# Transposing q, k and u by DMA transfers on SyncE's queue in a fused ALiBi sliding-window attention and MLP-mixer kernel

## The chip, the cores and the metric

The kernel runs on one core of a Trainium2 chip. The metric is the device time of one execution in microseconds. Three runs of the kernel before took 337.27, 339.14 and 339.30 us; the median is 339.14 us. One further execution was profiled; every row of a trace in this document is from such a profiled execution.

## The reference

For 8 batches of 576 tokens, 8 heads of 64, an attention with a window of 128 keys and a linear distance penalty per head is followed by an MLP mixer over the heads' joined output x (576 x 512 per batch):

```python
scores = scale * np.matmul(q, k.transpose(0, 1, 3, 2))
mask = (rel >= 0) & (rel < window)            # rel = query position - key position, window = 128
scores = np.where(mask, scores + bias[None], -1000000000.0)
attn = np.exp(scores - max); attn = attn / (sum(attn) + 1e-09)
x = np.matmul(attn, v)                        # heads joined: 512 columns
h = np.maximum(xt @ w_tok1, 0.0) @ w_tok2     # xt = x transposed: mixes the 576 tokens through 256
u = x + h.transpose(0, 2, 1)
out = u + np.maximum(u @ w_ch1, 0.0) @ w_ch2  # mixes the 512 channels through 1536
```

## The kernel before

**Blocks.** Two batches form a pair `pr` with nine blocks of 128 tokens: blocks 0 to 3 are the first batch's first 512 tokens, 4 to 7 the second's, and block 8 (`TAIL`) holds the last 64 tokens of both. They are loaded and prepared in the order `ORDER = [0, 1, 2, 3, 7, TAIL, 4, 5, 6]` (L97), 36 blocks in all (`todo`). A batch with an even number attends blocks 0, 1, 2, 3 and TAIL, one with an odd number 4 to 7.

**Loads.** `load` (L80 to L95) fetches a block of q, k and v from memory on GpSimd's (POOL's) queue, cast from f32 to bf16 on the way, with tokens on partitions and heads times 64 in the row. q and k go to rings `qld` and `kld` of 12 buffers each (pool `ld`, L55), v to a ring of 14. `load_to(n + 7)` keeps the issue seven blocks ahead of the block that is being prepared.

**Preparing a block.** Scores need the head dimension on partitions. `transposes` (L190 to L202) turns a block of q and k with eight TensorE transpositions (L195: four squares of 128 x 128 of q, four of k, two heads in each) into one PSUM tile `tp` of pool `ps_o`, which has one buffer (L64), and one VectorE copy (L201) brings it to `qkT` in SBUF (pool `tp` of 8 buffers, L56).

**Attention.** A unit is one block of queries. `scores` (L204 to L234) makes 8, 16 or 24 matmuls into two PSUM tiles `sp` (L219), one for each group of four heads, each from a pool of one buffer (L63): 8 for blocks 0 and 4, which have no earlier keys; 24 for TAIL. ScalarE takes the exponential (L228), VectorE multiplies with a mask that carries the distance penalty (L231). `values` (L236 to L258) multiplies with v for one group of heads into `ot` (L252), again in the one buffer of `ps_o`, and VectorE divides by the sums (L255, L257) into `xb`. `attention` (L262 to L287) runs the units, with the values of a unit behind the scores of the next one.

**Token mix.** `token_mix` (L292 to L335) makes `t1` (L303), its relu on ScalarE (L305), `ht` for each block (L321) and u = x + h on VectorE (L322). Then every block of u is transposed with four TensorE transpositions (L327) into `ut` (pool `ps_o`) and copied by VectorE (L333) to `uT`, or `uTt` for TAIL.

**Channel mix.** `channel_mix` (L338 to L375) makes 12 tiles `ct` with four matmuls each (L347), all of which read `uT` of all four blocks, with a relu on ScalarE (L349); for an odd batch also three `cx` for TAIL (L356) after every fourth `ct`. Then, for each block, 12 matmuls into `o2` (L365, named `o` in the trace), the addition of u on VectorE (L369) into `ob` (three buffers, L61), and a store on SyncE's (SP's) queue (L374, or two halves for TAIL, L372).

**The order of the work.** Attention and token mix of batch 0 run alone. Then, for each batch, `interleave` (L386 to L398) lays the channel mix of batch b and the attention and token mix of batch b + 1 (`side`, L377) into one another. Every `yield` states the cost of a step in nominal ns (450 for a prepared block, 700 for the scores of a unit, 300 for the values of one head group, 225 for a transposed block of u, 864 for a `ct`); as much side work is laid as 0.78 of the channel mix's cost. The framework makes each engine's queue from this, with the waits between engines; the trace shows that it also sets ready matmuls of one group between those of another, so that the queue's order is the listed order only in the large. The last batch's channel mix has no side work beside it.

Of the kernel before, what the change touches and what calls it, by code (L numbers as in the profile page):

```python
# [11 lines left out]
BF16 = mybir.dt.bfloat16  # L12
# [4 lines left out]
def kernel(  # L17
# [15 lines left out]
    nc = tc.nc  # L33
    P = nc.NUM_PARTITIONS
# [9 lines left out]
    NHP = H // 2  # L44
    NJ = DTOK // P
    NCB = DM // P
# [5 lines left out]
    HEADS = [[0, 2, 4, 6], [1, 3, 5, 7]]  # L52

    const = ctx.enter_context(tc.tile_pool(name="const", bufs=1))
    ld = ctx.enter_context(tc.tile_pool(name="ld", bufs=12))  # L55
    tpool = ctx.enter_context(tc.tile_pool(name="tp", bufs=8))  # L56
    ppool = ctx.enter_context(tc.tile_pool(name="pp", bufs=3))
    small = ctx.enter_context(tc.tile_pool(name="small", bufs=4))
    xpool = ctx.enter_context(tc.tile_pool(name="xp", bufs=2))
# [4 lines left out]
    ps_o = ctx.enter_context(tc.tile_pool(name="ps_o", bufs=1, space=PS))  # L64
    ps_m = ctx.enter_context(tc.tile_pool(name="ps_m", bufs=3, space=PS))

    ident = const.tile([P, P], BF16, name="ident")
# [27 lines left out]
        return got  # L95

    ORDER = [0, 1, 2, 3, 7, TAIL, 4, 5, 6]  # L97
    todo = [(pr, blk) for pr in range(B // 2) for blk in ORDER]
    loaded = {}

    def load_to(n):
        while len(loaded) < min(n, len(todo)):
            key = todo[len(loaded)]
            loaded[key] = load(*key)
# [82 lines left out]
    qkT = {}  # L187
    xs = {}

    def transposes(pr, blk):  # L190
        got = loaded[pr, blk]
        tp = ps_o.tile([P, 2 * NHP, P], BF16, name="tp", tag="o")
        for i, t in enumerate(("q", "k")):
            for hp in range(NHP):
                nc.tensor.transpose(  # L195
                    tp[:, i * NHP + hp, :],
                    got[t][:, 2 * hp : 2 * hp + 2, :].rearrange("p h d -> p (h d)"),
                    ident[:, :],
                )
        t = tpool.tile([P, 2 * NHP, P], BF16, name="qkT", tag="qkT")  # L200
        nc.vector.tensor_copy(out=t[:, :, :], in_=tp[:, :, :])  # L201
        qkT[pr, blk] = t  # L202

    def scores(pr, blk):  # L204

        tail = blk == TAIL
        first = 0 if tail or blk % NC else 1
        me = qkT[pr, blk]
        sp = [ps_s[e].tile([P, 4, 2, P], F32, name=f"sp{e}", tag="s") for e in range(2)]

        work = [(1, blk, 0, P)]
        if tail:
            work += [(0, NC - 1, 0, R), (0, 2 * NC - 1, R, P)]
        elif not first:
            work += [(0, blk - 1, 0, P)]
        for i in range(4):
            for kind, kb, c0, c1 in work:
                for e in range(2):
                    nc.tensor.matmul(  # L219
                        sp[e][:, i, kind, c0:c1],  # L220
                        lhsT=qkT[pr, kb][e * D : (e + 1) * D, NHP + i, :],
                        rhs=me[e * D : (e + 1) * D, i, c0:c1],
                        start=True, stop=True,
                    )
        pb = []
        for e in range(2):
            pe = ppool.tile([P, 4, 2, P], BF16, name=f"pe{e}", tag=f"pe{e}")
            nc.scalar.activation(out=pe[:, :, first:, :], in_=sp[e][:, :, first:, :],  # L228
                                 func=ACT.Exp, scale=scale)
            mk = (maskt if tail else masks)[e]  # L230
            nc.vector.tensor_tensor(out=pe[:, :, first:, :], in0=pe[:, :, first:, :],  # L231
                                    in1=mk[:, :, first:, :], op=ALU.mult)
            pb.append(pe)
        return pb  # L234
# [27 lines left out]
    def attention(b):  # L262
        pr, half = b // 2, b % 2
        if half == 0:
            xs[pr] = xpool.tile([P, NB, DM], BF16, name="xb", tag="xb")
        units = SCORE_ORDER[half]
        trs = [ORDER[:6], ORDER[6:]][half]
        n = pr * NB + (6 if half else 0)
        wait = list(trs)
        held = None  # L270
        for u in units + [None]:
            need = [] if u is None else ([u, 2 * NC - 1] if u == TAIL else [u])
            while any((pr, w) not in qkT for w in need):
                t = wait.pop(0)
                n += 1
                load_to(n + 7)
                transposes(pr, t)
                yield 450
            got = None
            if u is not None:  # L280
                got = (u, scores(pr, u))
                yield 700
            if held is not None:
                for e in range(2):
                    values(pr, held[0], e, held[1][e])
                    yield 300
            held = got  # L287


    us, uts, r1s = {}, {}, {}  # L290

    def token_mix(b):  # L292
        pr, half = b // 2, b % 2
        xb = xs[pr]
        if half == 0:
            us[pr] = xpool.tile([P, NB, DM], BF16, name="ub", tag="ub")
        blocks = list(range(half * NC, (half + 1) * NC))
        r1 = rpool.tile([P, NJ, DM], BF16, name="r1", tag=f"r1{half}")
        for j in range(NJ):
            t1 = ps_m.tile([P, DM], F32, name="t1", tag="m")  # L300
            ks = [(c, blocks[c]) for c in range(NC)] + [(NC + half, TAIL)]
            for n, (c, blk) in enumerate(ks):
                nc.tensor.matmul(t1[:, :], lhsT=W1[:, c, j * P : (j + 1) * P], rhs=xb[:, blk, :],  # L303
                                 start=n == 0, stop=n == len(ks) - 1)
            nc.scalar.activation(out=r1[:, j, :], in_=t1[:, :], func=ACT.Relu)  # L305
            yield 1080
        r1s[pr, half] = r1
        uT = rpool.tile([P, NCB, NC * P], BF16, name="uT", tag="uT")
        uTt = None
        if half:  # L310
            blocks.append(TAIL)
            uTt = rpool.tile([P, NCB, P], BF16, name="uTt", tag="uTt")
        for blk in blocks:
            ht = ps_m.tile([P, DM], F32, name="ht", tag="m")
            if blk == TAIL:
                mms = [(W2t[:, i, j, :], r1s[pr, i][:, j, :]) for i in range(2) for j in range(NJ)]
            else:
                c = blk % NC
                mms = [(W2[:, j, c * P : (c + 1) * P], r1[:, j, :]) for j in range(NJ)]
            for n, (l, r) in enumerate(mms):  # L320
                nc.tensor.matmul(ht[:, :], lhsT=l, rhs=r, start=n == 0, stop=n == len(mms) - 1)  # L321
            nc.vector.tensor_tensor(out=us[pr][:, blk, :], in0=ht[:, :], in1=xb[:, blk, :], op=ALU.add)  # L322
            yield 432
        for blk in blocks:
            ut = ps_o.tile([P, NCB, P], BF16, name="ut", tag="o")
            for cb in range(NCB):
                nc.tensor.transpose(ut[:, cb, :], us[pr][:, blk, cb * P : (cb + 1) * P], ident[:, :])  # L327
            if blk == TAIL:
                to = uTt[:, :, :]
            else:  # L330
                c = blk % NC
                to = uT[:, :, c * P : (c + 1) * P]
            nc.vector.tensor_copy(out=to, in_=ut[:, :, :])  # L333
            yield 225
        uts[b] = (uT, uTt)  # L335


# [39 lines left out]
    def side(b):  # L377

        yield from attention(b)
        yield from token_mix(b)  # L380
# [21 lines left out]
    load_to(9)  # L402
    load_channel_weights(1)
    drain(attention(0))
    drain(token_mix(0))
    for b in range(B):
        other = side(b + 1) if b + 1 < B else None
# [31 lines left out]
```

## Time and profile before

| | |
|---|---|
| runs | 337.27, 339.14, 339.30 us, median 339.14 us |
| profiled execution | 335.55 us, span of its instructions 333.8 us |
| mean granted TensorE clock | 0.987 |
| chain that ended last, by engine | PE 84%, DVE 7%, ACT 4%, issue 1%, DMA 1%, POOL 1% |
| q0, transfers issued by POOL | 116640 packets, 17.97 MB |
| q1, transfers issued by SP | 5248 packets, 9.44 MB |

How to read it. PE is TensorE's matmuls (transpositions among them), PEld its weight loads, DVE VectorE, ACT ScalarE, POOL GpSimd, SP SyncE. The span runs from the first to the last instruction; the execution's own time is 1.75 us longer. A row of the groups names a line, an engine and an operation, output and inputs by the program's names, the count, busy us and the mean of one in ns, and the idle time of the engine ahead of it with what ended it. A row of a timeline begins with the start and the duration in us; matmuls are pipelined, so durations of neighbours overlap, and the distance between starts is what a group takes. A table of stretches gives for each piece of the span the busy time of each engine with the count of instructions, the granted clock, and the load of the DMA engines. Answers on one tile end with the time from a transfer's issue to its landing.

### The profile page before, as it was taken

How to read it: one execution, taken by the hardware profiler on the slowest of the kernel's cores; microseconds unless marked ns; L12 is line 12 of the kernel's file. 1: busy time of each engine (PE TensorE's matmuls, PEld its weight loads, DVE VectorE, ACT ScalarE, POOL GpSimd, SP SyncE). 2: the span in 40 equal slices, each digit the busy share in tenths (PEclk: the TensorE clock that was granted, in tenths of full speed). 3: DMA queues.
4: the chain of work that ended last, by engine and by line, in shares of the span. 5: the costliest groups of instructions: out<-in, count | busy, mean ns of one | idle time of the engine just before them, and what ended most of it. 6: DMA issues, size and time to landing. Idle time of an engine off the chain costs nothing.

```text
span 333.8 us, 6457 instructions
## 1 busy us (share of the span) xinstructions
PE 303.6 (91%) x2688; PEld 162.6 (49%) x2688; DVE 169.7 (51%) x378; ACT 136.9 (41%) x213; POOL 111.0 (33%) x146
## 2 busy tenths in 40 slices
PE   2457769999999999999999999999999999999993
PEld 1234335545555555455565555455654555455541
DVE  2354456563665636474656546464656447461021
ACT  1653227702774038602863047504772057404600
POOL 8998565888786033303472000000000000000000
PEclk9999599999999999999999999999999999999998
DMA  9999999999999359914999220011000220011022
GB/s 74 136 114 167 170 195 161 139 117 189 174 105 131 75 110 77 67 44 101 73 85 83 81 78 3 0 63 66 2 2 13 83 63 2 0 65 63 2 76 82
DMA packets 121917, 27.81 MB, mean 83 GB/s; under 512 B 113824, under 2 KB 117280, under 8 KB 121888
## 3 DMA queue, kind: packets, MB, share of 16 engines
q0 software_dynamic: 116640, 17.97, 76.1%
q1 hardware_dynamic: 5248, 9.44, 8.2%
q8 instruction: 21, 0.34, 0.4%
q14 instruction: 8, 0.07, 0.1%
HBM read 35.91 MB, written 9.44 MB: 136 GB/s over the span
## 4 chain that ended last, share of the span: by engine, by line
PE 84%; DVE 7%; ACT 4%; issue 1%; DMA 1%; POOL 1%; POOLq 0%
PE o L365 28%; PE ct L347 23%; PE sp L219 7%; PE tp L195 6%; PE ot L252 6%; PE t L303 5%; PE ht L321 5%; PE cx L356 3%; PE ut L327 3%; ACT pe L228 2%; DVE xb L257 2%; DVE pe L231 2%; DVE ub L322 1%; DMA kld<-in_k_dram 1%; DVE qkT L201 1%
## 5 line engine op out<-in xcount | busy, mean ns | idle before, releaser
L349 ACT ACTIVATE r<-ct 128x512 bf16<-128x512 f32 x96 | 56.0, 601 | 133.9 <-PE ct L347 133.9
L347 PE MATMUL ct<-uT,WC 128*128 128x512 bf16 x384 | 98.0, 379 | 0.5 <-DVE uT L333 0.5
L365 PE MATMUL o<-WC,r 128*128 128x512 bf16 x384 | 95.4, 379 | 0.4
L228 ACT ACTIVATE pe<-sp 128x1024 bf16<-128x1024 f32 (+1 forms) x72 | 63.0, 926 | 27.3 <-PE sp L219 27.3
L365 PEld LDWEIGHTS <-r 128*128 128x128 bf16 x384 | 36.0, 98 | 37.6 <-issue 1.9
L91 POOL DMA_DIRECT2D qld<-in_q_dram x40 | 35.6, 891 | 45.3 <-PE tp L195 39.3
L369 DVE TENSOR_TENSOR ob<-o,ub 128x512 f32<-128x512 f32 x36 | 24.8, 690 | 48.1 <-PE o L365 48.1
L347 PEld LDWEIGHTS <-WC 128*128 128x128 bf16 x384 | 33.5, 98 | 28.0 <-issue 0.6
L231 DVE TENSOR_TENSOR pe<-pe,mask 128x1024 bf16<-128x1024 bf16 (+1 forms) x64 | 39.0, 619 | 12.1 <-ACT pe L228 8.0
L201 DVE COPY qkT<-tp 128x1024 bf16<-128x1024 bf16 x36 | 24.9, 692 | 31.5 <-PE tp L195 31.5
L94 POOL DMA_DIRECT2D v<-in_v_dram x40 | 35.0, 881 | 15.1 <-PE ot L252 6.2
L92 POOL DMA_DIRECT2D kld<-in_k_dram x40 | 35.4, 884 | 8.3 <-DMA WC<-in_moe_w_ch_dram 5.8
L322 DVE TENSOR_TENSOR ub<-ht,xb 128x512 bf16<-128x512 f32 x36 | 24.0, 688 | 27.1 <-PE ht L321 26.7
L252 PE MATMUL ot<-v,pe 128*128 128x65 bf16 (+1 forms) x544 | 30.4, 201 | 6.7 <-DVE pe L231 3.5
L252 PEld LDWEIGHTS <-pe 128*128 128x128 bf16 (+1 forms) x544 | 22.4, 102 | 26.6 <-DVE xb L257 17.1
L257 DVE TENSOR_TENSOR xb<-ot,rt 128x256 bf16<-128x256 f32 x72 | 30.6, 425 | 2.5
L219 PE MATMUL sp<-qkT 64*128 64x128 bf16 (+1 forms) x544 | 24.6, 224 | 4.0 <-DVE qkT L201 3.1
L255 DVE RECIPROCAL rt<-ot 128x4 f32<-128x4 f32 x72 | 12.9, 179 | 26.1 <-PE ot L252 25.5
L219 PEld LDWEIGHTS <-qkT 64*128 64x128 bf16 x544 | 17.6, 98 | 17.6 <-DVE qkT L201 16.6
L303 PE MATMUL t<-xb,W 128*128 128x512 bf16 x80 | 23.4, 402 | 0.8 <-DVE xb L257 0.8
L195 PE MATMUL tp<-ident,qld 128*128 128x128 bf16 x144 | 14.8, 228 | 9.1 <-DMA qld<-in_q_dram 5.0
L321 PE MATMUL ht<-r,W 128*128 128x512 bf16 x64 | 19.4, 398 | 0.3 <-ACT r L305 0.3
(46 smaller groups left out, 179.4 us busy)
## 6 DMA issues: line engine op xcount, KB each, us to landing
out_dram<-ob SPq DMA_DIRECT2D x32, 256.0 KB, 2.0
qld<-in_q_dram POOLq DMA_DIRECT2D x32, 128.0 KB, 5.5
kld<-in_k_dram POOLq DMA_DIRECT2D x32, 128.0 KB, 5.6
v<-in_v_dram POOLq DMA_DIRECT2D x32, 128.0 KB, 5.5
WC<-in_moe_w_ch_dram POOLq DMA_DIRECT2D x4, 768.0 KB, 10.4
out_dram<-ob SPq DMA_DIRECT2D x8, 128.0 KB, 2.3
qld<-in_q_dram POOLq DMA_DIRECT2D x8, 64.0 KB, 4.6
kld<-in_k_dram POOLq DMA_DIRECT2D x8, 64.0 KB, 4.2
```

The lines of the kernel that those rows point to most:

```text
L91: nc.gpsimd.dma_start(out=got["q"][p0 : p0 + n, :, :], in_=rows(q, b, s0, n))
L92: nc.gpsimd.dma_start(out=got["k"][p0 : p0 + n, :, :], in_=rows(k, b, s0, n))
L219: nc.tensor.matmul(sp[e][:, i, kind, c0:c1], lhsT=qkT[pr, kb][e * D : (e + 1) * D, NHP + i, :], rhs=me[e * D : (e + 1) * D, i, c0:c1], sta ...
L228: nc.scalar.activation(out=pe[:, :, first:, :], in_=sp[e][:, :, first:, :], func=ACT.Exp, scale=scale)
L231: nc.vector.tensor_tensor(out=pe[:, :, first:, :], in0=pe[:, :, first:, :], in1=mk[:, :, first:, :], op=ALU.mult)
L252: nc.tensor.matmul(ot[to, i, :], lhsT=l, rhs=r, start=m == 0, stop=m == len(mms) - 1, skip_group_check=True)
L257: nc.vector.tensor_tensor(out=x4[:, :, e, :], in0=ot[:, :, 0:D], in1=rt[:, :, :].broadcast_to([P, 4, D]), op=ALU.mult)
L303: nc.tensor.matmul(t1[:, :], lhsT=W1[:, c, j * P : (j + 1) * P], rhs=xb[:, blk, :], start=n == 0, stop=n == len(ks) - 1)
L321: nc.tensor.matmul(ht[:, :], lhsT=l, rhs=r, start=n == 0, stop=n == len(mms) - 1)
L347: nc.tensor.matmul(ct[:, :], lhsT=WC1[:, cb, t * P : (t + 1) * P], rhs=uT[:, cb, :], start=cb == 0, stop=cb == NCB - 1)
L349: nc.scalar.activation(out=r2[:, t, :], in_=ct[:, :], func=ACT.Relu)
L365: nc.tensor.matmul(o2[:, :], lhsT=l, rhs=WC2[:, t, :], start=t == 0, stop=t == NHT - 1)
```

## The change

Three things are edited.

1. The pool of loaded q and k goes from 12 to 9 buffers each, the pool of `qkT` from 8 to 11.
2. The first six blocks of the order are transposed on TensorE as before. For the other 30, `transpose_to(n + 4)` issues two transposing transfers on SyncE's queue, one for q and one for k, from the loaded tile straight to `qkT`, up to four blocks ahead of the block whose turn it is. For those blocks `transposes`, with its PSUM tile, its copy and its step of cost 450, is not called.
3. For all batches but the first, each block of u is transposed by one transfer on SyncE's queue from `ub` to `uT` or `uTt`; the four transpositions, the PSUM tile, the copy and the step of cost 225 go.

Stores stay on the same queue, and everything else is as it was.

```diff
@@ -52,8 +52,8 @@
     HEADS = [[0, 2, 4, 6], [1, 3, 5, 7]]
 
     const = ctx.enter_context(tc.tile_pool(name="const", bufs=1))
-    ld = ctx.enter_context(tc.tile_pool(name="ld", bufs=12))
-    tpool = ctx.enter_context(tc.tile_pool(name="tp", bufs=8))
+    ld = ctx.enter_context(tc.tile_pool(name="ld", bufs=9))
+    tpool = ctx.enter_context(tc.tile_pool(name="tp", bufs=11))
     ppool = ctx.enter_context(tc.tile_pool(name="pp", bufs=3))
     small = ctx.enter_context(tc.tile_pool(name="small", bufs=4))
     xpool = ctx.enter_context(tc.tile_pool(name="xp", bufs=2))
@@ -95,6 +95,7 @@
         return got
 
     ORDER = [0, 1, 2, 3, 7, TAIL, 4, 5, 6]
+    EARLY = 6
     todo = [(pr, blk) for pr in range(B // 2) for blk in ORDER]
     loaded = {}
 
@@ -200,6 +201,21 @@
         t = tpool.tile([P, 2 * NHP, P], BF16, name="qkT", tag="qkT")
         nc.vector.tensor_copy(out=t[:, :, :], in_=tp[:, :, :])
         qkT[pr, blk] = t
+
+    moved = [EARLY]
+
+    def transpose_to(n):
+
+        while moved[0] < min(n, len(todo)):
+            key = todo[moved[0]]
+            moved[0] += 1
+            t = tpool.tile([P, 2 * NHP, P], BF16, name="qkT", tag="qkT")
+            for i, x in enumerate(("q", "k")):
+                nc.sync.dma_start_transpose(
+                    out=t[:, i * NHP : (i + 1) * NHP, :],
+                    in_=loaded[key][x][:, :, :].rearrange("p h d -> p (h d)"),
+                )
+            qkT[key] = t
 
     def scores(pr, blk):
 
@@ -270,12 +286,14 @@
         held = None
         for u in units + [None]:
             need = [] if u is None else ([u, 2 * NC - 1] if u == TAIL else [u])
-            while any((pr, w) not in qkT for w in need):
+            while any(w in wait for w in need):
                 t = wait.pop(0)
                 n += 1
                 load_to(n + 7)
-                transposes(pr, t)
-                yield 450
+                transpose_to(n + 4)
+                if (pr, t) not in qkT:
+                    transposes(pr, t)
+                    yield 450
             got = None
             if u is not None:
                 got = (u, scores(pr, u))
@@ -322,16 +340,20 @@
             nc.vector.tensor_tensor(out=us[pr][:, blk, :], in0=ht[:, :], in1=xb[:, blk, :], op=ALU.add)
             yield 432
         for blk in blocks:
-            ut = ps_o.tile([P, NCB, P], BF16, name="ut", tag="o")
-            for cb in range(NCB):
-                nc.tensor.transpose(ut[:, cb, :], us[pr][:, blk, cb * P : (cb + 1) * P], ident[:, :])
             if blk == TAIL:
                 to = uTt[:, :, :]
             else:
                 c = blk % NC
                 to = uT[:, :, c * P : (c + 1) * P]
-            nc.vector.tensor_copy(out=to, in_=ut[:, :, :])
-            yield 225
+            if b == 0:
+                ut = ps_o.tile([P, NCB, P], BF16, name="ut", tag="o")
+                for cb in range(NCB):
+                    nc.tensor.transpose(ut[:, cb, :], us[pr][:, blk, cb * P : (cb + 1) * P],
+                                        ident[:, :])
+                nc.vector.tensor_copy(out=to, in_=ut[:, :, :])
+                yield 225
+            else:
+                nc.sync.dma_start_transpose(out=to, in_=us[pr][:, blk, :])
         uts[b] = (uT, uTt)
```

## The prediction, made before the result was known

> **What bounds the kernel now.** I read the page first, then the table of busy time by stretches, cut where each batch's channel mix begins (the first `ct` after the last `o`).
>
> ```profile
> span 333.8 us, 6457 instructions
> PE 303.6 (91%) x2688; PEld 162.6 (49%) x2688; DVE 169.7 (51%) x378; ACT 136.9 (41%) x213; POOL 111.0 (33%) x146
> DMA  9999999999999359914999220011000220011022
> ```
>
> ```profile
> core 0: us, PE busy (x) PEld busy (x) DVE busy (x) ACT busy (x) POOL busy (x), PEclk, DMA share, GB/s
> 0.00:46.50 46.50, 23.57 (x242) 14.58 (x243) 20.79 (x62) 16.17 (x29) 40.04 (x62) 0.93 1.61 138
> 46.50:80.10 33.60, 33.38 (x275) 17.14 (x275) 18.31 (x40) 14.46 (x22) 24.62 (x30) 1.00 2.07 153
> 80.10:120.90 40.80, 40.35 (x399) 22.23 (x398) 23.16 (x49) 17.98 (x27) 22.06 (x27) 1.00 1.52 128
> 120.90:154.30 33.40, 33.18 (x275) 17.04 (x274) 19.00 (x41) 14.46 (x22) 8.77 (x10) 1.00 0.73 72
> ...
> 302.70:333.80 31.10, 26.03 (x157) 13.03 (x154) 4.15 (x6) 8.96 (x15) 0.00 (x0) 0.97 0.15 51
> ```
>
> Three stages. Until 46.5 us PE is half idle: the first batch's attention and token mix run alone. From 46.5 to 302.7 seven channel mixes run with the next batch's attention and token mix between them, and PE is busy 98 to 99% of each (33.18 of 33.40). The last 26 us of work are a channel mix alone. So in the middle, 256 us, work taken off PE is worth its full time unless something else becomes late. DVE and ACT are about half busy there, and the granted clock is 1.00.
>
> **What is removed from PE.** One timeline of PE in the third channel mix gives both kinds of transposition, and a wait that matters below.
>
> ```profile
> 121.58 0.39 PE L195 MATMUL tp<-ident,qld 128*128 128x128 bf16 x4
> 121.80 0.39 PE L195 MATMUL tp<-ident,kld 128*128 128x128 bf16 x4
> 122.03 1.03 PE L347 MATMUL ct<-uT,WC 128*128 128x512 bf16 x4
> ...
> 130.39 0.62 PE L219 MATMUL sp<-qkT 64*128 64x128 bf16 x16
> 130.94 0.42 PE L252 MATMUL ot<-v,pe 128*128 128x65 bf16 x8
> ...
> 132.44 1.19 PE L219 MATMUL sp<-qkT 64*128 64x128 bf16 x16
> 133.56 0.42 PE L252 MATMUL ot<-v,pe 128*128 128x65 bf16 x8
> ...
> 146.47 0.39 PE L327 MATMUL ut<-ident,ub 128*128 128x128 bf16 x4
> 146.69 0.81 PE L365 MATMUL o<-WC,r 128*128 128x512 bf16 x3
> ```
>
> Durations overlap, so I count from start to start. A block of q and k takes PE from 121.58 to 122.03, 0.45 us for eight transpositions; a block of u 146.47 to 146.69, 0.22 us for four. Removed are 30 blocks of q and k (36 less the first six) and 32 of u (36 less batch 0's four): 30 x 0.45 + 32 x 0.22 = 13.5 + 7.0 = **20.5 us**, nearly all between 46.5 and 302.7. An upper bound comes from the chain that ended last:
>
> ```profile
> PE o L365 28%; PE ct L347 23%; PE sp L219 7%; PE tp L195 6%; PE ot L252 6%; PE t L303 5%; PE ht L321 5%; PE cx L356 3%; PE ut L327 3%; ACT pe L228 2%; DVE xb L257 2%; DVE pe L231 2%; DVE ub L322 1%; DMA kld<-in_k_dram 1%; DVE qkT L201 1%
> ```
>
> 6% of 333.8 us x 30/36 plus 3% x 32/36 is 16.7 + 8.9 = 25.6 us; that holds the slow first six blocks too, so I keep 20.5.
>
> **What is removed from DVE.** The copies out of PSUM:
>
> ```profile
> L201 DVE COPY qkT<-tp 128x1024 bf16<-128x1024 bf16 x36 | 24.9, 692 | 31.5 <-PE tp L195 31.5
> L333 DVE COPY uT<-ut 128x512 bf16<-128x512 bf16 x32 | 13.5, 422 | 9.2 <-PE ut L327 9.2
> ```
>
> 30 x 0.692 + 32 x 0.42 = 34 us of DVE. I cost it at nothing: DVE is half idle in the middle, and PE's waits there (0.2 to 0.45 us per stretch) leave almost nothing to win. The tiles `tp` and `ut` also leave the single buffer of ps_o to `ot`.
>
> **A wait that comes back.** The two groups of `sp` above are alike, sixteen matmuls each. The first takes 0.55 us from start to start (130.39 to 130.94); the second, the only full unit of its batch with no block transposed ahead of it, takes 1.12 (132.44 to 133.56). ACT shows why:
>
> ```profile
> 131.04 1.94 ACT L228 ACTIVATE pe<-sp 128x1024 bf16<-128x1024 f32 x2 [0.60 <-PE sp L219]
> 132.87 0.60 ACT L349 ACTIVATE r<-ct 128x512 bf16<-128x512 f32 x1
> 133.62 1.94 ACT L228 ACTIVATE pe<-sp 128x1024 bf16<-128x1024 f32 x2 [0.15 <-PE sp L219]
> ```
>
> Scores have one buffer per head group; the exponentials of the unit before hold it until 131.04 + 1.94 = 132.98, and PE waits in the middle of its group, counted as busy. It costs 0.57 us. Without blocks of 0.45 us between, and with the steps of cost 450 gone so that less channel mix is laid between two units, every full unit can meet it. Full units are three per odd batch (one pays already) and four per even batch: 4 x 2 + 3 x 4 = 20 new ones, at most 20 x 0.57 = 11.4 us. The lower bound is zero: other ready matmuls can fill the place. I take the middle, **5.7 us**.
>
> **What is added on SP's queue.** 30 x 2 + 32 = 92 transposing transfers of 128 x 512 bf16, 128 KB each, among the 40 stores. The trace has no such transfer. Nearest are SP's own stores:
>
> ```profile
> L374 SPq DMA_DIRECT2D out_dram<-ob x3: 333/337/378, 70.7 to 78.3; - x3
> ...
> DMA to landing us min/median/max: 5.8/5.9/6.1
> ```
>
> ```profile
> L374 SPq DMA_DIRECT2D out_dram<-ob x4: 332/332/333, 183.3 to 193.3; - x4
> L372 SPq DMA_DIRECT2D out_dram<-ob x2: 473/530/588, 195.9 to 196.4; - x2
> ...
> DMA to landing us min/median/max: 2.0/2.0/2.4
> ```
>
> The first answer is for 46 to 80 us, while loads fill the DMA engines; the second for 160 to 200 us. An issue holds SP 0.33 to 0.59 us and lands after 2.0 us in quiet time, 5.9 us among loads. Bounds for what one transfer costs the queue: 0.33 us (issue only, transfers overlap) to 5.9 us (one at a time, among loads). The store of the shared block shows two issues at 195.9 and 196.4 us, the second before the first can have landed, so transfers of this queue overlap; I take a holding time well under 2 us and a landing of 2 to 6 us.
>
> Is that covered? A pair of batches takes 74.2 us now (33.4 + 40.8) and would take about 68; it carries 27 transfers and ten stores. At 2.0 us one after another that is 54 + 4 us, still inside. Latency comes from PE's timeline:
>
> ```profile
> 144.96 1.03 PE L321 MATMUL ht<-r,W2t 128*128 128x512 bf16 x4
> 145.82 0.81 PE L365 MATMUL o<-WC,r 128*128 128x512 bf16 x3
> ...
> 154.14 1.03 PE L347 MATMUL ct<-uT,WC 128*128 128x512 bf16 x4
> ...
> 156.41 0.40 PE L219 MATMUL sp<-qkT 64*128 64x128 bf16 x8
> ...
> 174.33 0.63 PE L219 MATMUL sp<-qkT 64*128 64x128 bf16 x24
> ```
>
> Blocks of q and k are issued four ahead of their use. The tightest is within an even batch's attention: block 7 is issued with unit 0 (156.41) and used by the shared unit (174.33), 18 us later; less six blocks on PE (2.7 us) and their lost steps (6 x 450 / 0.78 = 3.5 us), 12 us remain for the four transfers in front. For u, this batch's last `ht` ends at 145.82, 8.5 us before the next channel mix; the lost steps end the side work 3 x 450 / 0.78 = 1.7 us earlier and five `ut` (1.1 us) go, so about 9 us remain. The last transfers alone have to fit there, since each block starts as it is ready. Queued behind a late transfer are the stores; `ob` has three buffers at 2.6 us of `o` each. Price in the middle: zero.
>
> The Trainium skill speaks against this. "VectorE: DVE Perf Modes", The three transpose paths, gives 1309 ns for 128 x 128 through DMA against 390 ns on TensorE; the trace disagrees on the latter, at 55 ns from start to start here. If the former were a rate, a transfer of four squares would take an estimated 5.2 us, 92 of them 482 us, and the kernel would be far slower. "DMA: Bandwidth & Descriptors", Latency and other measured facts, gives 261 GB/s for transposing transfers, an estimated 0.5 us each and 46 us in all, which would leave everything covered. No run here shows either yet.
>
> **Loads, and the start.** The ring of q and k loads shrinks from 12 to 9 buffers, and a load now waits for a transfer on SP nine blocks back instead of PE's work twelve back.
>
> ```profile
> L195 PE MATMUL tp<-ident,qld x144: 216/219/314, 4.8 to 277.6; 128*128 128x128 bf16 x144
> L91 POOL DMA_DIRECT2D qld<-in_q_dram x40: 677/881/1607, 1.3 to 174.0; - x40
> ...
> DMA to landing us min/median/max: 2.5/5.2/12.2
> ```
>
> The last load is issued at 174.0 us and used at 277.6, so loads have up to 100 us of lead and I cost the ring at nothing. Only the start is tight: the ninth block of the order (its k issued at 37.49 us) lands by 49.7 us at the worst 12.2, and two transfers at 5.9 us can end at 61 us, where the scores that use it stand at 56.17 us today.
>
> ```profile
> 37.49 0.87 POOL L92 DMA_DIRECT2D kld<-in_k_dram  x1 [2.86 <-DMA WC<-in_moe_w_ch_dram]
> ...
> 56.17 0.62 PE L219 MATMUL sp<-qkT 64*128 64x128 bf16 x16
> ```
>
> That is 0 to 5 us; channel-mix matmuls fill part of it. I take **1.5 us**.
>
> **The sum.** The profiled execution took 335.55 us (span 333.8). 335.55 - 20.5 + 5.7 + 1.5 = 322.3 us. The median shown, 339.14, lies 3.6 above that execution, so on its scale **326 us**, 4% less.
>
> **The rivals.** *Full gain.* Other matmuls fill every place and the start costs nothing: 335.55 - 20.5 = 315.1, on the median's scale 319; with the chain's 25.6, 314. For it: PE idles 2 us in all of the middle. Against: the 1.12 us group.
>
> *ACT takes the bound.* All 20 units pay 0.57 us and the start its 5 us: 335.55 - 20.5 + 11.4 + 5 = 331.5, on the median's scale 335; with a shortage like it at token mix as well, 336 to 338, no change to be told. For it: exponentials of a full unit hold ACT 1.94 us, and the lost steps crowd them. Against: ACT is 43% busy in those stretches.
>
> *The queue becomes the bound (slower).* Transposing transfers go one at a time on SP. Then a pair of batches needs 27 t + 4 us, and it is slower than before once that passes 74.2 us, from t = 2.6 us. At t = 3.9 us, midway between the stores' 2.0 and 5.9, 92 transfers and 40 stores of 0.4 us take 375 us; from 38 us, when the first loads concerned have landed, and with the last channel mix of 31 us behind them, 38 + 375 + 31 = 444 us. For it: 5.9 us among loads, DMA engines at 90% or more for the first 117 us. Against: the overlapping stores, and loads that end at 174 us. The Trainium skill's 1309 ns (same page and section as above) is this case by rule: an estimated 38 + 482 + 16 + 31 = 567 us.
>
> *It does not do what it says:* the transfers' waits on SP reorder PE's work so that nothing is gained; nothing in the profile speaks for it.
>
> **Chances.** Forecast 0.55 (its own range 320 to 333 us), full gain 0.16, ACT 0.13, the queue 0.14, the last 0.02. A measurement of this kernel tells about 1% from no change, 335.7 to 342.5 us. Faster by more: 0.55 + 0.16 = 0.71; within: 0.13 + 0.02 = 0.15; slower: 0.14. The range 314 to 342 us leaves out the queue's case and a little below: under 0.2.
>
> **What would show it.** Right: PE's `tp` falls to 48 matmuls and `ut` to 16, the even and odd stretches shorten from 33.4 and 40.8 us to about 32 and 38, PE stays above 95% busy there, SP's queue waits for DVE more than for its own transfers. The ACT term: groups of sixteen `sp` of about 1.1 us at most full units. Wrong: PE waiting for DMA at `sp` or at the first `ct` of a batch, transfers landing one behind the other at over 2.6 us, or stores issued late. A shorter first 46.5 us would also be unforeseen, since nothing there changes.

## The result, and the profile after

The changed kernel is slower: 359.19 us median (358.64 to 359.56) against 338.31 (337.27 to 339.3) for the kernel before in the same comparison, a ratio of 1.062 (95% interval 1.057 to 1.066). The forecast was 326 us. The profiled execution took 359.56 us, against 335.55 before. One of the four executions of the last kernel below ran in a slower state of the chip (332.42 us), and its figures are those of the other three.

The page of the changed kernel, the lines that answer to those of before:

```profile
span 357.8 us, 5827 instructions
PE 290.5 (81%) x2279; PEld 150.4 (42%) x2320; DVE 138.4 (39%) x316; ACT 137.4 (38%) x213; POOL 110.7 (31%) x146
PEclk9999555669985699999999999999999999999999
DMA  9999999999999999999993993312300331043012
...
L369 PE MATMUL ct<-uT,WC 128*128 128x512 bf16 x364 | 99.1, 393 | 17.2 <-DMA uT<-ub 15.1
L235 PE MATMUL sp<-qkT 64*128 64x128 bf16 (+1 forms) x544 | 33.1, 233 | 19.6 <-DMA qkT<-kld 15.8
```

PE has 13 us less to do (303.6 to 290.5) and waits much longer. Waits for transfers are new: 15.1 us at one `ct`, and 15.8 us in three waits at `sp`. The DMA engines are full for the first 21 of the 40 slices instead of the first 13, and the granted clock falls to 0.5 to 0.6 in two places (slices of 8.9 us: from 36 to 80 us, and from 107 to 125). Where the time goes is plain from the same table of stretches as before, cut at each batch's channel mix:

```profile
core 0: us, PE busy (x) PEld busy (x) DVE busy (x) ACT busy (x) POOL busy (x), PEclk, DMA share, GB/s
0.00:72.40 72.40, 29.98 (x295) 18.53 (x300) 23.72 (x68) 21.18 (x35) 49.72 (x73) 0.78 1.80 138
72.40:117.60 45.20, 29.90 (x171) 13.13 (x175) 11.51 (x26) 9.87 (x16) 26.90 (x33) 0.80 1.98 153
117.60:157.10 39.50, 38.39 (x329) 20.25 (x336) 17.63 (x39) 18.05 (x27) 21.04 (x26) 0.95 2.02 164
157.10:188.30 31.20, 30.79 (x227) 15.08 (x230) 15.36 (x33) 14.51 (x22) 9.01 (x11) 1.00 1.71 168
188.30:226.30 38.00, 36.91 (x330) 19.99 (x334) 17.63 (x39) 17.91 (x27) 4.04 (x5) 1.00 0.64 98
...
```

From 157 us on the kernel is what was forecast: stretches of 31.2 and 38.0 us where 33.4 and 40.8 stood. The loss lies ahead of that. The first channel mix begins at 72.4 us instead of 46.5 (+25.9), and the first stretch after it contains the wait of 15.1 us. From each kernel's first channel mix to its end, without that wait, the changed kernel is 17.0 us shorter (270.3 against 287.3 us; the expectations below say 16.8). 335.55 + 25.9 + 15.1 - 17.0 = 359.55 us: this is bookkeeping from the two traces, not a check of their causes. A part of the 25.9 us is work moved and not time lost: the first stretch holds 295 matmuls where it held 242, scores of batch 1 that came behind it before.

PE's timeline shows both losses, and, further on, a wait that the prediction had named:

```profile
24.96 0.63 PE L321 MATMUL t<-xb,W 128*128 128x512 bf16 x1 [6.24 <-DMA W<-in_moe_w_tok_dram]
...
49.92 0.39 PE L235 MATMUL sp<-qkT 64*128 64x128 bf16 x2 [10.02 <-DMA qkT<-kld]
...
56.84 0.71 PE L235 MATMUL sp<-qkT 64*128 64x128 bf16 x10 [3.48 <-DMA qkT<-kld]
...
62.30 1.03 PE L235 MATMUL sp<-qkT 64*128 64x128 bf16 x8 [2.26 <-DMA qkT<-kld]
63.27 2.74 PE L339 MATMUL ht<-r,W 128*128 128x512 bf16 x6
...
72.36 1.01 PE L369 MATMUL ct<-uT,WC 128*128 128x512 bf16 x2 [0.51 <-DVE uT L353]
...
117.59 1.87 PE L369 MATMUL ct<-uT,WC 128*128 128x512 bf16 x4 [15.14 <-DMA uT<-ub]
...
159.31 1.09 PE L235 MATMUL sp<-qkT 64*128 64x128 bf16 x16
```

*The start.* The `sp` of 49.92, 56.84 and 62.30 us belong to batch 1, and they stand on PE's queue ahead of batch 0's `ht` (63.27). Before, batch 1's scores came behind batch 0's last `ut`. The scores wait for transferred blocks, 15.8 us in all, and the rest of batch 0's token mix waits behind them. The fourth wait, of a `t` for its weights (6.2 us), is no wait for a transfer: the first of those is issued only at 39.75 us. Here this `t` stands on PE's queue ahead of the scores of block 2; before, it stood behind those of block 3 and did not wait:

```profile
26.47 1.74 PE L303 MATMUL t<-xb,W 128*128 128x512 bf16 x4
```

All six kernels with six early blocks have this wait, of 5.9 to 6.3 us, and none with nine or more. So it comes with another order of PE's queue; why that order changed stays open. The four waits add up to 22.0 of the 25.9 us.

*The wait for u.* What SP does meanwhile is on its own timeline, and DVE's shows when u was ready:

```profile
39.75 1.30 SPq L214 DMA_TRANSPOSE qkT<-qld  x1
41.11 1.26 SPq L214 DMA_TRANSPOSE qkT<-kld  x1
...
102.32 1.25 SPq L214 DMA_TRANSPOSE qkT<-qld  x1
104.10 1.37 SPq L214 DMA_TRANSPOSE qkT<-kld  x1
105.56 6.02 SPq L356 DMA_TRANSPOSE uT<-ub  x4
111.67 1.25 SPq L356 DMA_TRANSPOSE uTt<-ub  x1
113.01 1.56 SPq L396 DMA_DIRECT2D out_dram<-ob  x3
```

```profile
93.63 0.69 DVE L340 TENSOR_TENSOR ub<-ht,xb 128x512 bf16<-128x512 f32 x1 [0.17 <-PE ht L339]
94.93 0.69 DVE L391 TENSOR_TENSOR ob<-o,ub 128x512 f32<-128x512 f32 x1 [0.60 <-PE o L387]
...
119.71 0.69 DVE L391 TENSOR_TENSOR ob<-o,ub 128x512 f32<-128x512 f32 x1 [18.91 <-DMA out_dram<-ob]
```

Batch 1's last u (`TAIL`'s) is ready at 94.3 us, and the transfers of all five blocks are issued from 105.56 on. The first `ob` is ready at 95.6 and its store goes out at 113.01; the fourth `ob` waits 18.9 us for a buffer. From its first transfer at 39.75 us to 105.56, 65.8 us, SP issues 28 transfers of q and k, which hold it 40.6 us in all. Most of the rest it stands at transfers whose blocks have not been loaded:

```profile
SPq L214 <- DMA qld<-in_q_dram: 60.7, 9, 39.1
```

Of these waits (us in total, times, longest), 39.1 us pass ahead of its first transfer, and 21.6 us at eight later ones. The holding alone would not have made u late: an estimate of 28 x 1.3 us from 39.75 on ends at 76 us, before u is there. The order of SP's queue, as its timeline shows it, q and k transfers counted together, then u's, then stores:

```
28 q/k | 5 u | 4 stores | 10 q/k | 4 u | 6 stores | 8 q/k | 5 u | 4 stores | 10 q/k | ...
```

Fourteen blocks, not four, are queued ahead of the first u. They are blocks 6 to 19 of the order, as far as eleven buffers go: block 19 takes over the buffer of block 8, the last of the first pair.

### The profile page after: what moved, and what is told of

Read it like the earlier page. It is cut to its first block, busy times and chain, and to the rows that moved or that the text cites. A ratio compares the mean times of both kernels' runs of the same rounds, so it can differ in the third digit from the quotient of the medians.

```text
span 357.8 us, 5827 instructions
## 1 busy us (share of the span) xinstructions
PE 290.5 (81%) x2279; PEld 150.4 (42%) x2320; DVE 138.4 (39%) x316; ACT 137.4 (38%) x213; POOL 110.7 (31%) x146
## 3 DMA queue, kind: packets, MB, share of 16 engines
q1 hardware_dynamic: 55296, 21.51, 34.1%
## 4 chain that ended last, share of the span: by engine, by line
PE 57%; DMA 19%; POOL 7%; issue 5%; ACT 5%; DVE 4%; SPq 3%; ACTq 0%; POOLq 0%
PE o L387 23%; PE ct L369 16%; DMA qld<-in_q_dram 7%; DMA kld<-in_k_dram 5%; PE ht L339 4%; DMA qkT<-kld 4%; ACT pe L244 4%; PE sp L235 4%; PE ot L268 4%; PE t L321 4%; PE cx L378 2%; DMA uT<-ub 2%; DVE pe L247 2%; POOL v L94 2%; SPq L214 2%
## 5 line engine op out<-in xcount | busy, mean ns | idle before, releaser
L369 PE MATMUL ct<-uT,WC 128*128 128x512 bf16 x364 | 99.1, 393 | 17.2 <-DMA uT<-ub 15.1
L371 ACT ACTIVATE r<-ct 128x512 bf16<-128x512 f32 x96 | 57.1, 605 | 144.4 <-PE ct L369 143.9
L387 PE MATMUL o<-WC,r 128*128 128x512 bf16 x375 | 84.2, 379 | 0.3
L387 PEld LDWEIGHTS <-r 128*128 128x128 bf16 x384 | 37.5, 98 | 45.1
L369 PEld LDWEIGHTS <-WC 128*128 128x128 bf16 x384 | 34.1, 100 | 52.3 <-issue 20.2
L235 PE MATMUL sp<-qkT 64*128 64x128 bf16 (+1 forms) x544 | 33.1, 233 | 19.6 <-DMA qkT<-kld 15.8
L91 POOL DMA_DIRECT2D qld<-in_q_dram x40 | 34.8, 869 | 25.4 <-DMA qkT<-kld 8.1
L235 PEld LDWEIGHTS <-qkT 64*128 64x128 bf16 x544 | 22.1, 102 | 37.0 <-DMA qkT<-kld 17.7
L321 PE MATMUL t<-xb,W 128*128 128x512 bf16 x73 | 22.0, 399 | 7.4 <-DMA W<-in_moe_w_tok_dram 6.2
L378 PE MATMUL cx<-uTt,WC 128*128 128x128 bf16 x192 | 13.2, 219 | 0.0
L378 PEld LDWEIGHTS <-WC 128*128 128x128 bf16 x192 | 11.8, 98 | 2.8
```

The lines of the kernel that those rows point to most:

```text
L91: nc.gpsimd.dma_start(out=got["q"][p0 : p0 + n, :, :], in_=rows(q, b, s0, n))
L235: nc.tensor.matmul(sp[e][:, i, kind, c0:c1], lhsT=qkT[pr, kb][e * D : (e + 1) * D, NHP + i, :], rhs=me[e * D : (e + 1) * D, i, c0:c1], sta ...
L369: nc.tensor.matmul(ct[:, :], lhsT=WC1[:, cb, t * P : (t + 1) * P], rhs=uT[:, cb, :], start=cb == 0, stop=cb == NCB - 1)
L371: nc.scalar.activation(out=r2[:, t, :], in_=ct[:, :], func=ACT.Relu)
L387: nc.tensor.matmul(o2[:, :], lhsT=l, rhs=WC2[:, t, :], start=t == 0, stop=t == NHT - 1)
```

## The experiments

The theories that the expectations speak of, in short. **A**: two separate losses, each tied to its own blocks (the blocks that batch 1's first scores need, and batch 1's u); put those back on TensorE and the loss goes. **B**: the loss is a property of the loaded queue, and takes another form when one block is taken out of it. **A2**, formed after the first four runs: SP's queue stands still at q and k transfers whose loads have not come, and whatever was put behind them (u, stores) is late; on PE the same happens at batch 1's scores; only the order has to change. All ratios are against the kernel before on the same chip; its medians there lie between 337.69 and 338.86 us.

| kernel | median us | ratio (95%) | q/k ahead of first u or store | 1st, 2nd, 3rd channel mix at us |
|---|---|---|---|---|
| before | 338.31 | | none | 46.5, 79.9, 120.7 |
| changed | 359.19 | 1.062 (1.057 to 1.066) | 28 | 72.4, 117.6, 157.1 |
| u only | 335.38 | 0.990 (0.986 to 0.994) | 0 | 47.3, 86.0, 127.4 |
| q and k only | 361.77 | 1.071 (1.069 to 1.074) | 28 | 72.8, 104.2, 153.9 |
| nine early | 354.82 | 1.051 (1.047 to 1.055) | 22 | 47.9, 113.9, 152.9 |
| nine early, u from batch 2 | 346.73 | 1.026 (1.023 to 1.029) | 22 | 48.0, 85.7, 143.2 |
| SP ordered | 343.56 | 1.013 (1.008 to 1.018) | 14 | 69.5, 97.1, 140.0 |
| PE ordered | 358.41 | 1.058 (1.054 to 1.062) | 28 | 54.3, 116.8, 156.3 |
| both ordered | 334.95 | 0.990 (0.985 to 0.994) | 14 | 52.7, 87.9, 131.3 |
| nine early, SP ordered | 327.37 | 0.966 (0.960 to 0.972) | 8 | 49.0, 86.3, 124.1 |
| pools of before | 347.76 | 1.029 (1.023 to 1.034) | 22 | 70.1, 105.3, 144.4 |
| eighteen early, SP ordered | 326.18 | 0.965 (0.959 to 0.971) | 0 | 48.5, 83.4, 123.2 |
| nine early, SP ordered, pools of before | 327.49 | 0.971 (0.963 to 0.979) | 8 | 49.5, 85.9, 125.1 |

**u only.** All 36 blocks of q and k on TensorE, pools as before; u of batches 1 to 7 by transfers.

```diff
-    EARLY = 6
+    EARLY = 36
```

> Only the blocks of u go by transfers; all 36 blocks of q and k are transposed on TensorE, with the pools of before (12 and 8). Theory A (the loss comes from the order in which the queues were filled: at the start PE's queue holds batch 1's scores, which wait for transfers, ahead of batch 0's remaining work, and SP's queue holds eleven blocks of q and k ahead of batch 1's u): neither is left, the first channel mix starts at 46.5 us as before, the second does not wait, and 32 x 0.22 = 7.0 us are saved: 335.5 - 7 = about 328.5 us in the profiled execution. Theory B (a transposing transfer among loads is late in itself, wherever it stands in the queue): batch 1's u still lands late and the second channel mix waits more than 5 us, 334 us or more.

Measured 335.38 us, 2.3 us less than before on that chip and not the 7 of A. The time lies in B's range, though the wait, 3.8 us, is under B's 5. SP's timeline, then DVE's and PE's, at batch 1's u:

```profile
71.70 4.06 SPq L356 DMA_TRANSPOSE uT<-ub  x3
...
76.59 1.51 SPq L356 DMA_TRANSPOSE uT<-ub  x1
78.15 2.14 SPq L356 DMA_TRANSPOSE uTt<-ub  x1
```

```profile
73.86 0.68 DVE L340 TENSOR_TENSOR ub<-ht,xb 128x512 bf16<-128x512 f32 x1
```

```profile
86.01 1.12 PE L369 MATMUL ct<-uT,WC 128*128 128x512 bf16 x4 [3.82 <-DMA uT<-ub]
```

Here no transfer of q or k is ahead of u. The fourth block of u, the last that `ct` needs, is ready at 74.5 us; its transfer goes out at 76.59, behind the three before it and one store, and PE still waits until 86.01, 9.4 us later. Among loads, then, the transfers alone cost 3.8 us at the first u, on a queue with nothing else late.

**q and k only.** u stays on TensorE in every batch.

```diff
-            if b == 0:
+            if True:
```

> Only q and k go by transfers, from block 7 on; u is transposed on TensorE in all batches. Theory A: the start stays late by about 26 us, the 15.1 us wait for u is gone, and the 7.0 us of u's transposition come back: 359.5 - 15.1 + 7.0 = about 351 us. Theory B: the DMA engines are what is short, so that the wait moves from u to the scores of batch 2, 356 us or more.

The expected saving of 15 us did not come: 361.77 us, in B's range. No `ct` waits for u, but the same 28 transfers stand ahead of the stores, `ob` runs out, and PE waits for DVE:

```profile
L369 PE MATMUL ct<-uT,WC 128*128 128x512 bf16 x364 | 99.4, 393 | 9.2 <-DVE ob L391 7.2
```

The second stretch between channel mixes is 49.7 us long. This is against A; but the wait is at the stores, and not at batch 2's scores, where B had put it.

**Nine early.** Blocks 6 to 8 of the order, which batch 1 scores first, go back to TensorE.

```diff
-    EARLY = 6
+    EARLY = 9
```

> The first nine blocks (both batches of the first pair) are transposed on TensorE, the rest as in the change. Theory A: PE's queue at the start is that of before, so the first channel mix starts at 46.5 us, 26 us earlier than in the change, for 3 x 0.45 us more on PE; 22 transfers of q and k still stand ahead of batch 1's u, so up to 15 us of that wait may stay: 320 to 335 us, near the upper end if the wait is whole. Theory B: the start is late because loads and transfers share the DMA engines, so less than half of the 26 us comes back: 345 us or more.

The start is back at 47.9 us, as A has it, yet the total is 354.82, in B's range and not in A's, for another reason than B's: the wait for u doubles.

```profile
113.89 1.44 PE L369 MATMUL ct<-uT,WC 128*128 128x512 bf16 x3 [29.08 <-DMA uT<-ub]
```

The 22 transfers ahead of u wait for the loads of the same last blocks: those of u are issued from 101.30 us on, against 105.56. PE is there at 84.8 us instead of 102.5, and u comes at 113.9 instead of 117.6.

**Nine early, u from batch 2.** In addition batch 1's u stays on TensorE.

```diff
-    EARLY = 6
+    EARLY = 9
...
-            if b == 0:
+            if b <= 1:
```

> As the run with nine early blocks, and batch 1's u on TensorE too. Theory A: no long wait is left, and the stages from the second channel mix on are as short as in the change (31.3 and 38.0 us against 33.4 and 40.8): 335.5 - 5 x about 2.4 - 2.9 = about 320.5 us. Theory B: waits of more than 5 us for transfers among loads remain at the second or third channel mix, 328 us or more.

346.73 us. The start (48.0) and the second channel mix (85.7) are in place, and then the stores hold everything, as PE's, SP's and DVE's timelines show:

```profile
106.99 1.87 PE L369 MATMUL ct<-uT,WC 128*128 128x512 bf16 x4 [17.96 <-DVE ob L391]
```

```profile
99.64 7.66 SPq L396 DMA_DIRECT2D out_dram<-ob  x4
```

```profile
75.77 0.68 DVE L391 TENSOR_TENSOR ob<-o,ub 128x512 f32<-128x512 f32 x1
...
106.25 0.69 DVE L391 TENSOR_TENSOR ob<-o,ub 128x512 f32<-128x512 f32 x1 [22.21 <-DMA out_dram<-ob]
```

The first `ob` is ready at 76.5 us and its store is issued at 99.64. Three times the loss has moved to the next thing behind the same transfers. A in its first form fell, and A2 took its place.

**SP ordered, PE ordered, both.** SP: each q or k transfer is queued behind the store or u transfer that the program lists ahead of it. PE: batch 1's scores are queued behind batch 0's last `ut`. No work is changed.

```diff
+    def behind(ins):
+        return nullcontext() if ins is None else tc.issue_after(ins)
...
-                nc.sync.dma_start_transpose(
+                with behind(queued[0]):
+                    nc.sync.dma_start_transpose(
...
-                got = (u, scores(pr, u))
+                with behind(turned[0] if b == 1 else None):
+                    got = (u, scores(pr, u))
```

`queued[0]` is set at every store and u transfer, `turned[0]` at every `ut` transposition.

> The change whole, with one thing added: each transfer of q and k is queued on SP behind the store or transfer of u that the program lists before it, so that 14 transfers of q and k instead of 28 stand ahead of batch 1's u. Theory A2 (SP's queue stands still at transfers of blocks whose loads have not come, and u and the stores stand behind them): the start stays as late as in the change (72 us), the 15.1 us wait at the second channel mix goes to under 3: 359.5 - 15 = about 345 us. Theory B (transposing transfers among loads are slow by themselves): 8 us or more of that wait stay, 352 us or more.

> The change whole, with one thing added: on PE, batch 1's scores are queued behind the last transposition of batch 0's u. Theory A2: the first channel mix starts before 52 us instead of 72, but the SP queue still reaches batch 1's u only when the loads of block 20 of the order have come, near 106 us as in the change, so the second channel mix starts near 115 us again and the time stays within 4 us of the change: 355 to 360 us. Theory C (the late start is the loss, and the wait for u follows from it): 359.5 - 20 = 340 us or less.

> The change whole with both queues ordered: batch 1's scores behind batch 0's u on PE, and transfers of q and k behind the stores and transfers of u listed before them on SP. Theory A2: both losses go, the short stages of the change stay (31.3 and 38.0 us): 335.5 - 16.8 + 2 to 8 for batch 1's blocks, whose loads come late = 320 to 328 us. Theory B: waits of more than 10 us for transfers among loads remain, 333 us or more.

SP's order alone gave 343.56 us, 15.6 us less than the changed kernel, as A2 had it: the second channel mix begins without a wait, and the start remains (69.5 us).

```profile
97.12 1.03 PE L374 MATMUL ct<-uT,WC 128*128 128x512 bf16 x4
```

PE's order alone gave 358.41, within the expected range: the start goes to 54.3 us (expected before 52), and the wait for u grows to 26.6, because the 28 transfers still stand ahead of u, which is issued from 104.66 us on.

```profile
116.75 1.87 PE L374 MATMUL ct<-uT,WC 128*128 128x512 bf16 x4 [26.64 <-DMA uT<-ub]
```

The two together gave 334.95, 24 us less than the changed kernel, but 7 us above A2's range and inside B's, though no wait of over 10 us is left. Fourteen transfers are still ahead of u, `sp` still waits 7.7 us in all for transfers, and the second stretch takes 43.5 us. The wait of the `t` for its weights is there too, and is most of the 6.2 us by which the start (52.7) is later than before:

```profile
PE t L328 <- DMA W<-in_moe_w_tok_dram: 5.9, 1, 5.9
```

**Nine early, SP ordered.**

> Nine early blocks on TensorE, and transfers of q and k queued on SP behind what the program lists before them, so that eight of them stand ahead of batch 1's u (22 in the run with nine early blocks). Theory A2: neither wait is left: 335.5 - 16.8 + 3 x 0.45 = about 320 us, up to 325 with small waits. Theory B: a wait of 8 us or more at the second channel mix, 330 us or more.

327.37 us, 3.4% less than before, between A2's range and B's. Eight transfers are ahead of u, and 2.6 us of its wait remain:

```profile
86.26 1.02 PE L374 MATMUL ct<-uT,WC 128*128 128x512 bf16 x4 [2.60 <-DMA uT<-ub]
```

The third and fourth stretches are 31.3 and 41.1 us where 31.3 and 38.0 were to be.

**Pools of before.** The changed kernel with `ld` of 12 and `tp` of 8 buffers.

```diff
-    ld = ctx.enter_context(tc.tile_pool(name="ld", bufs=9))
-    tpool = ctx.enter_context(tc.tile_pool(name="tp", bufs=11))
+    ld = ctx.enter_context(tc.tile_pool(name="ld", bufs=12))
+    tpool = ctx.enter_context(tc.tile_pool(name="tp", bufs=8))
```

> The changed kernel with the pools of before (loads' ring 12, eight blocks of transposed q and k instead of eleven). PE's order stays as in the changed kernel; on SP's queue 22 transfers of q and k, not 28, stand ahead of the first of u. Theory A2 (the queue stands still at transfers whose loads haven't come, and u and the stores stand behind it; the number ahead is set by the eleven buffers): the first channel mix still starts at 70 to 73 us, the wait for u at the second falls from 15 to 2 to 8 us, total 345 to 353 us. Rival C (each transfer among loads is simply slow, and the order counts for little): wait 12 us or more, total 356 us or more.

347.76 us. Eight buffers let eleven blocks ahead of u instead of fourteen, the transfers of u are issued at 93.33 us instead of 105.56, and the wait halves, all as A2 has it:

```profile
105.28 1.87 PE L369 MATMUL ct<-uT,WC 128*128 128x512 bf16 x4 [7.38 <-DMA uT<-ub]
```

So the enlarged pool of `qkT` made the loss larger: it is what let the queue run so far ahead.

**Eighteen early, SP ordered.** u by transfers from batch 2 on (`b <= 1` on TensorE), 18 blocks of q and k on TensorE, SP ordered: no transfer until 89 us.

> Eighteen blocks of q and k stay on TensorE, u goes by transfers from the third batch on, and each q and k transfer is queued behind the store or transfer of u listed before it: no transfer until most loads are in. Theory A2: what is left of the loss in the kernel with nine early blocks and the same order (2.6 us of waiting for u, a first stage of 37.3 us and a later one of 41.1) is transfers among loads; without them the start is 46 to 48 us, the first two stages are as before (33.5 and 40.5) and the later ones 31.3 and 38, total 321 to 326 us. Rival D (what counts is how many transpositions leave TensorE): 9 blocks x 0.45 + 4 x 0.22 = 5 us are given back, total 330 us or more.

326.18 us, at the upper edge of A2's 321 to 326 and below D's 330; the start (48.5) is a little outside A2's 46 to 48. Its stretches:

```profile
0.00:48.50 48.50, 26.49 (x242) 16.46 (x243) 21.00 (x62) 16.20 (x29) 40.87 (x62) 1.00 1.58 137
48.50:83.40 34.90, 34.63 (x275) 17.68 (x275) 18.31 (x40) 14.46 (x22) 24.23 (x29) 0.96 2.05 149
83.40:123.20 39.80, 39.48 (x386) 21.53 (x385) 21.59 (x45) 17.98 (x27) 18.11 (x22) 1.00 1.41 131
123.20:155.20 32.00, 31.84 (x252) 15.71 (x251) 17.06 (x36) 14.62 (x22) 14.01 (x16) 1.00 1.63 143
155.20:193.30 38.10, 37.65 (x335) 20.02 (x334) 17.62 (x39) 17.91 (x27) 13.74 (x17) 1.00 1.55 141
```

PE is busy about 99% of each from 48.5 us on, one wait of 0.3 us for a transfer is left, and the stage of 41.1 us is 38.1. Moving 13 blocks fewer costs nothing against the kernel with nine early blocks, so what those blocks save on PE is lost elsewhere there; the waits among loads account for some of it (2.6 us for u, 1.9 us at one `sp` of the 41.1 us stage). The start and the first stretch are 2.0 and 1.3 us longer than before; why was not found.

**Nine early, SP ordered, pools of before.** Both pool sizes as in the previous pool experiment.

> The kernel with nine early blocks and the queue's order, with the pools of before (loads' ring 12, eight transposed blocks). If the smaller ring costs nothing, as predicted: within 1% of 327.4 us. If the ring of nine delays loads: 322 us or less, with the stages of 37.3 and 41.1 us shortened. If eight transposed blocks are too few: over 331 us, with PE waiting for qkT at sp.

327.49 us, within 1% of 327.37: the two pool sizes, changed together, count for nothing once the queue's order is held. The stage of 41.1 us is 38.0 here, though transfers stand among loads as before, while the one of 37.9 takes 39.2; so the length of a single stage in one profiled execution is weak evidence.

## Why the prediction was wrong, point by point

**The step that failed** is the price of zero for what is added on SP's queue, with its ground, "Blocks of q and k are issued four ahead of their use". It took the program's listed order for the queue's order. The queue ran fourteen blocks ahead, to the limit of the `qkT` buffers, though the kernel's description had said that the listed order holds only in the large. An in-order queue that starts late work early stands still there. That this order makes most of the loss is shown by the runs that hold it: ordering SP's queue alone gives 15.6 us back, both queues 24 of the 33 us between forecast and measurement, with the same 92 transfers. For the 9 us that are left, the trace with both queues ordered shows two waits, 7.7 us at `sp` for transfers among loads and 5.9 us of the `t`; no run parts them.

The profile of before could have priced it. The timeline of its POOL queue has the load of the twentieth block, the last one queued ahead of u:

```profile
79.69 0.89 POOL L92 DMA_DIRECT2D kld<-in_k_dram  x1 [0.24 <-issue]
```

With the 5.2 us of a median load it lands at about 85 us, when the second channel mix had already begun at 79.9; only then could batch 1's u and the first store have gone out. That is 5 us plus the transfers themselves, and nothing in the prediction asked when SP could leave that place. The price would still have been too low: beside the transfers this load is issued later, at 92.46 us in the changed kernel and at 88.02 with nine early blocks.

**The start, 1.5 us, bounds 0 to 5.** It cost 25.9. The prediction looked at the one wait of batch 1's scores for the ninth block, and let channel-mix matmuls fill it. But those cannot start before batch 0's token mix, which was now queued behind these scores. With nine early blocks the start is 47.9 us. Of the 22 us of waits, 15.8 belong to the transfers of blocks 6 to 8, and 6.2 to the `t` ahead of its weights, a change of PE's order that the prediction did not foresee.

**The landing, "2 to 6 us".** Right in quiet, too short among loads. Two answers on the q and k transfers, 200 to 334 us and 40 to 100 us:

```profile
L214 SPq DMA_TRANSPOSE qkT<-kld x5: 1206/1217/1873, 199.5 to 234.1; - x5
...
DMA to landing us min/median/max: 2.4/3.6/4.5
```

```profile
L214 SPq DMA_TRANSPOSE qkT<-kld x12: 1188/1254/5629, 41.1 to 96.9; - x12
...
DMA to landing us min/median/max: 6.8/7.2/14.6
```

The upper bound of 5.9 us was a store's. The "about 9 us" of cover for u (its "8.5 us" are 8.3 by the rows shown) were 7.7 in the u-only kernel (the fourth block of u ready at 74.5 us, PE free for its `ct` at 82.2), and the way from there to PE took 11.5, hence its 3.8 us of waiting.

**The holding time, "well under 2 us".** Right: 1.2 us (median), 1.3 from start to start, 5.6 at the most. Transfers overlap, so the rival in which the queue becomes the bound, one at a time from t = 2.6 us, did not happen, though its signs did (PE waiting for DMA at `sp` and at a first `ct`, stores issued late). The 1309 ns per square of the Trainium skill, "VectorE: DVE Perf Modes", The three transpose paths, is not a rate here: four squares hold SP for 1.2 us. The 261 GB/s of "DMA: Bandwidth & Descriptors", Latency and other measured facts, also from the Trainium skill, which the page gives for a non-contiguous middle dimension, were not reached: 128 KB in 1.3 us are 101 GB/s. The rival given 0.02, that the transfers' waits reorder PE's work, named one half of the loss, but not the order of SP's own queue, and put the time at no change. The profile did speak for it: the trace of before shows ready matmuls set between others.

**The PE saving, 20.5 us, and the wait that comes back, 5.7 us.** Right, where no transfer is late. A pair of stretches takes 31.2 + 38.0 = 69.2 us instead of 74.2, 5.0 less. Removed are 9 x 0.45 + 9 x 0.22 = 6.0 us per pair, so about 1 us came back, near 4 us over the 3.5 pairs. The group of 16 `sp` at 159.31 us with its 1.09 us is one of these waits. DVE has 31.3 us less to do (169.7 to 138.4), near the 34; no run separates what that is worth.

**The ring of loads at nothing.** Right, by the last experiment, as far as a run that also changes the other pool can show it.

**The low clock.** In the changed kernel the granted clock is 0.78 and 0.80 in the first two stretches, 0.93 and 1.00 before, and it is low around PE's long waits (10.0 us before 49.92, 15.1 us before 117.59). The Trainium skill, "TensorE: Matmul & The Clock Gate", Part 1: The HAM clock gate, has the clock halve after an idle window of about 3.4 us; the trace agrees for the 15.1 us (0.8 in the slice in which the wait begins, 0.5 in the next). For the 10.0 us it does not show the cause: the clock is 0.50 already from 36.5 to 39.9 us, where that wait begins, and PE had waited no longer than 1.3 us at a time since 25 us. What the low clock added by itself was not measured apart.

## What to carry to other kernels

Before work is moved to a queue that serves in order, ask how far that queue can run ahead (the output buffers set it, not the distance written in the program), and for each place of it when its input comes and who stands behind. Here the next batch's input and the stores went out 11 to 23 us after they were ready. With each transfer held behind the store or transfer listed ahead of it, the same idea brought 3.4% with nine blocks left on TensorE, and 3.5% when it also began only as the loads thin out.

## What the runs showed of the hardware

A transposing transfer of 128 x 512 bf16 holds SP 1.2 us, almost four times the 0.33 us of a store of a whole block, and lands after 2.4 us at the least. The 92 of them added 50048 packets to SP's queue (5248 to 55296), 544 each. Loads beside them become slow, here the loads of q in the changed kernel:

```profile
L91 POOL DMA_DIRECT2D qld<-in_q_dram x40: 679/883/1080, 1.3 to 169.8; - x40
...
DMA to landing us min/median/max: 3.4/9.8/19.7
```

9.8 us (median) stand against 5.2 before. With SP ordered it is 7.1, with nine early blocks and SP ordered 9.5, and with the ring of twelve (pools of before) 11.1; with eighteen, when the transfers begin at 89 us, 4.8, with the ring of nine; with u alone 5.6. So it goes with the q and k transfers among the loads, not with the ring. Whether their number of packets or their path is what slows the loads was not tried.
